# Last layer of a three-stage kernel: the Newton operations one turn later, conversions spread over the turns, row sums a turn earlier

## The chip, the core and the metric

The kernel runs on one core of a Trainium2 chip. The metric is the device time of one execution in microseconds; the time before is the median of three runs. A core has engines that run side by side and wait for one another through semaphores: TensorE (PE; PEld is its weight load), VectorE (DVE), ScalarE (ACT), GpSimd (POOL), and SyncE (SP), which here only issues transfers. Each engine works through its own list of instructions in the order in which the program gives them.

## What is computed

Attention with a window, a mixture of eight experts on its output, and a last dense layer on that. All the changes are in the last layer, which for 1536 tokens of width 512 computes

```
h = x @ w_in                                             # 512 -> 2048
sp = np.where(h > 20.0, h, np.log1p(np.exp(np.minimum(h, 20.0))))
g = h * np.tanh(sp)
out = g @ w_out                                          # 2048 -> 512
```

The inputs x are the sums of two rows per token that the experts left in memory, each with its weight. The weights w_in and w_out come as 64-bit numbers and are turned on the chip into pairs of a high and a low part; likewise every operand of a product has a high and a low part (`whi`/`wlo`, `xgh`/`xgl`, `hhi`/`hlo`), and a product is three matmuls (high by high, high by low, low by high).

## The kernel before

**Tiling.** The last layer takes the tokens in four blocks (`tb`) of 384 (`TB`) and the 2048 hidden columns in 16 pieces (`f`) of 128. A pair (tb, f) is a step; there are 64, numbered from 0. `last_in` does a step's first product: 12 matmuls of 384 columns into a PSUM tile `hp`, of which there are three. `last_out` does its second product: six matmuls with `hhi` and three with `hlo`, of 512 columns, added up over the 16 steps of a block in three PSUM tiles `ac`.

**Between the two products** a step has a chain on ScalarE and VectorE: `mish_0` Exp of hp into v (L1178, ScalarE); `mish_1` a minimum that keeps v in range (L1182, VectorE), Square into s (L1183) and Ln into r (L1184), both ScalarE; `mish_2` Exp of -r (L1188, ScalarE), a first value of a reciprocal; `mish_3` three operations on VectorE (L1193 to L1195), one Newton step and the product with h; below they are the Newton trio. `mish_5` copies the result into `hhi` (L1198, ScalarE) and `mish_6` takes the low part `hlo` (L1201, VectorE).

**Order.** The order is written out by hand: the loop at L1243 makes 66 turns, and each engine's list follows the code. Turn n emits the first product of step n, the second product of step n-2, and from the chain L1178, L1182 to L1188 and the trio of step n together with the copy and the low part of step n-1. The first and last step are cut in thirds.

**Work beside it.** In turns 2 to 13 the last six halves of weights are converted, one half in two turns: L327 and L328 in the even turn, L329 and L330 in the odd one, and at the end of the odd turn `rest` with a copy on ScalarE (L322) and L323 and L324 on VectorE. In blocks 0 to 2 the next block's inputs are made: GpSimd gathers the rows (`rows_of`, L868), `combine_2` scales one on ScalarE (L1153) and adds the other on VectorE (L1154), in turns f = 5, 9, 13; `combine_3` transposes the sum on TensorE (L1159) and splits it into high (L863, ScalarE) and low (L864, VectorE), in turns f = 6, 10, 14. All of that stands at the end of its turn, behind the trio. After a block `last_store` copies the results out (L1236 on ScalarE, L1234 on VectorE).

**Line numbers** are those of the kernel before; in the changed kernel these operations stand 8 to 10 lines further on (L1154 is L1164 there, L1193 is L1203, L864 is L874, and the conversion's L327, L328, L329, L330, L322, L323, L324 are L335, L336, L337, L338, L327, L330, L331).

Of the kernel before, what the change touches and what calls it, by code (L numbers as in the profile page):

```python
# [21 lines left out]
P = 128  # L22
# [154 lines left out]
def build(tc, ctx, I, out, n_global, n_local, dbg=None):  # L177
# [118 lines left out]
    def w64_load():  # L296
        j, s = divmod(state["load64"], 2)
        if j < 16:
            state["load64"] += 1
            raws[j, s] = wraw.tile([P, 512, 2], I32, name="raw")  # L300
            nc.sync.dma_start(raws[j, s], I["w_moe2"][j, :, s * 512:(s + 1) * 512].bitcast(I32)
                              .rearrange("p (a b) -> p a b", b=2))

    def w64_begin():


        j, s = divmod(state["conv"], 2)
        if j == 16:
            return None
        state["conv"] += 1  # L310
        if s == 0:
            pool, n = (wlast, "l") if j < 16 - RING else (wring, "")
            pieces[64 + j] = (pool.tile([P, 1024], F32R, name="whi" + n), pool.tile([P, 1024], F32R, name="wlo" + n))
        raw = raws.pop((j, s))
        lw, uw = raw[:, :, 0], raw[:, :, 1]
        hi, lo = (w[:, s * 512:(s + 1) * 512] for w in pieces[64 + j])
        t1 = wtmp.tile([P, 512], I32, name="t1", bufs=2)
        t2 = wtmp.tile([P, 512], I32, name="t2", bufs=1)
        f1 = t1.bitcast(F32)

        def rest():
            A.activation(hi, f1, AF.Copy)  # L322
            V.tensor_tensor(f1, f1, hi.bitcast(F32), op=OP.subtract)  # L323
            V.tensor_tensor(lo, f1, lo.bitcast(F32), op=OP.add)  # L324

        return (
            lambda: V.tensor_scalar(t1, uw, 0x07FFFFFF, 3, op0=OP.bitwise_and, op1=OP.logical_shift_left),  # L327
            lambda: V.scalar_tensor_tensor(t1, uw, -0x40000000, t1, op0=OP.bitwise_and, op1=OP.bitwise_or),  # L328
            lambda: V.tensor_scalar(t2, t1, -0x800000, None, op0=OP.bitwise_and),  # L329
            lambda: V.scalar_tensor_tensor(lo, lw.bitcast(U32), 2.0 ** -52, t2.bitcast(F32), op0=OP.mult, op1=OP.mult),  # L330
            rest,  # L331
        )

    xgs, xgT = {}, {}
# [836 lines left out]


    def mish_begin(hp, n):
        r = mk.tile([P, TB], F32, name="r", bufs=1)
        return hp, vt[:, n % 2, :TB], vt[:, 2 + n % 2, :TB], r

    def mish_0(m, cc):
        A.activation(m[1][:, cc], m[0][:, cc], AF.Exp)  # L1178
# [11 lines left out]
    def mish_3(m, cc):  # L1190

        h, v, s, r = (a[:, cc] for a in m)
        V.scalar_tensor_tensor(s, s, 1.0, r, op0=OP.add, op1=OP.mult)  # L1193
        V.scalar_tensor_tensor(s, s, -2.0, r, op0=OP.add, op1=OP.mult)
        V.scalar_tensor_tensor(v, s, 0.5, h, op0=OP.add, op1=OP.mult)  # L1195

    def mish_5(m, g, cc):
        A.activation(g[0][:, cc], m[1][:, cc], AF.Copy)  # L1198

    def mish_6(m, g, cc):  # L1200
        V.tensor_tensor(g[1][:, cc], m[1][:, cc], g[0][:, cc].bitcast(F32), op=OP.subtract)  # L1201

    def mish_end():  # L1203
        return tuple(mk.tile([P, CAP], F32R, name=n)[:, :TB] for n in ("hhi", "hlo"))
# [4 lines left out]
    def for_cuts(n, stage, *a):  # L1209

        for cc in (THIRDS if n in (0, 16 * NTB - 1) else [ALL]):
            stage(*a, cc)
# [26 lines left out]

    steps = [(tb, f) for tb in range(NTB) for f in range(16)]  # L1240
    m = {}
    vt = mk.tile([P, 4, CAP], F32, name="yT", bufs=1)
    for n in range(len(steps) + 2):  # L1243
        new, old = n < len(steps), 1 <= n <= len(steps)
        if new:
            tb, f = steps[n]
            m[n] = mish_begin(last_in(tb, f), n)
        if n >= 2:
            last_out(*steps[n - 2])
        if n % 2 == 0:  # L1250
            half = w64_begin() if n else None
        if new:
            for_cuts(n, mish_0, m[n])
        if old:
            g = gT[steps[n - 1]] = mish_end()
        if old:
            for_cuts(n - 1, mish_5, m[n - 1], g)
        if new:
            for_cuts(n, mish_1, m[n])
        if half:  # L1260
            half[n % 2 * 2]()
        if new:
            for_cuts(n, mish_2, m[n])
        if old:
            for_cuts(n - 1, mish_6, m[n - 1], g)
        if half:
            half[n % 2 * 2 + 1]()
        if new:
            for_cuts(n, mish_3, m[n])
        if late and n:  # L1270
            late.pop(0)()
        if half and n % 2:
            half[4]()
        if n >= 2:
            last_store(*steps[n - 2])
        if new and tb + 1 < NTB:
            for c in range(TC):
                t = TC * (tb + 1) + c
                if f == 2 + 4 * c:
                    rows[t] = [rows_of(t, 0), rows_of(t, 1)]  # L1280
                if f == 5 + 4 * c:
                    combine_2(t, rows[t])
                if f == 6 + 4 * c:
                    combine_3(t, rows[t], ps_q, "tq")
        if n % 2:
            w64_load()

# [107 lines left out]
```

## Time and profile before

| | us |
|---|---|
| median of 3 runs | 741.88 (741.67 to 742.07) |
| the profiled execution: its time | 742.57 |
| its span in the trace | 740.8 |
| TensorE busy, whole span | 707.8 (96%) |
| VectorE busy | 524.5 (71%) |
| ScalarE busy | 421.7 (57%) |

The span is what the trace covers of the profiled execution; its own time is 1.8 us more. Times below count from the span's start. Busy time of TensorE says that a matmul was under way; where matmuls follow each other closely they overlap in the trace, so the pace is read from their starts. The last layer begins at 444.86 us and takes the last 40% of the span.

### The profile page before, as it was taken

What the parts mean: (1) busy time and instruction counts of PE and PEld (TensorE: products, weight loads), DVE (VectorE), ACT (ScalarE), POOL (GpSimd) and SP (SyncE); (2) the same over time, 40 slices, a digit from 0 to 9 for tenths busy, and PEclk for the clock granted to TensorE, in tenths of its full rate; (3) what the DMA queues carried; (4) which work ended last, traced back from release to release, by engine and by line L of the source; (5) the groups of instructions that cost most, each with busy time, mean ns of one, the idle gap of its engine ahead of it and who ended that gap; (6) DMA issues with size and microseconds to landing.
All of it is one profiled execution on the core that took longest, in us unless ns stands there. A gap on an engine that the chain in (4) does not pass through costs nothing.

```text
span 740.8 us, 11706 instructions
## 1 busy us (share of the span) xinstructions
PE 707.8 (96%) x4259; PEld 642.3 (87%) x4259; DVE 524.5 (71%) x1237; ACT 421.7 (57%) x892; POOL 64.0 (9%) x83
## 2 busy tenths in 40 slices
PE   7999899999999999999999999898999999999994
PEld 4777778899999999999999988787989989989993
DVE  7789769877676675857576886888666666666653
ACT  5999632435354444444354447566767677676663
POOL 2000200301011010101000032100020020000000
PEclk9999899999999999999999999899999999999998
DMA  7799421757565565646454643300120030001001
GB/s 163 205 230 240 125 66 42 227 163 229 160 213 165 197 199 167 193 151 220 140 195 142 213 160 130 116 29 0 47 83 1 0 104 12 0 1 43 2 0 47
DMA packets 42932, 89.26 MB, mean 120 GB/s; under 512 B 5987, under 2 KB 18403, under 8 KB 42868
## 3 DMA queue, kind: packets, MB, share of 16 engines
q1 hardware_dynamic: 35412, 69.37, 30.7%
q0 software_dynamic: 4096, 13.11, 6.0%
q10 hardware_dynamic: 3360, 5.97, 2.2%
q8 instruction: 35, 0.57, 0.3%
q14 instruction: 29, 0.24, 0.1%
HBM read 75.32 MB, written 13.11 MB: 119 GB/s over the span
## 4 chain that ended last, share of the span: by engine, by line
PE 72%; DVE 14%; ACT 8%; issue 2%; DMA 2%; POOL 1%; ACTq 0%; DVEq 0%
PE hp L858 10%; PE hp L859 10%; PE hp L860 10%; PE ac L859 5%; PE ac L858 5%; PE ac L860 5%; PE ac L1222 5%; PE ac L1223 5%; PE ac L1227 4%; PE xp L567 3%; PE sp L516 3%; PE tp L554 3%; DVE wlo L280 2%; PE tq L892 2%; ACT r L1184 1%
## 5 line engine op out<-in xcount | busy, mean ns | idle before, releaser
L858 PE MATMUL hp<-xgh,whi 128*128 128x416 f32 (+1 forms) x288 | 104.3, 362 | 0.0
L860 PE MATMUL hp<-xgh,wlo 128*128 128x416 f32 (+1 forms) x288 | 100.8, 350 | 0.0
L859 PE MATMUL hp<-xgl,whi 128*128 128x416 f32 (+1 forms) x288 | 100.6, 349 | 0.2 <-DVE xgl L711 0.2
L280 DVE TENSOR_TENSOR wlo<-raw,whi 128x1024 fp32r<-128x1024 f32 x61 | 74.7, 1224 | 35.9 <-ACT whi L277 35.3
L858 PE MATMUL ac<-hhi,whi 128*128 128x416 f32 x256 | 91.7, 358 | 0.0
L859 PE MATMUL ac<-hlo,whi 128*128 128x416 f32 x256 | 90.0, 352 | 1.2 <-DVE hlo L905 1.2
L860 PE MATMUL ac<-hhi,wlo 128*128 128x416 f32 x256 | 89.9, 351 | 0.0
L1193 DVE SCALAR_TENSOR_TENSOR yT<-yT,r 128x384 f32<-128x384 f32 (+1 forms) x68 | 36.4, 535 | 73.8 <-ACT r L1188 69.8
L858 PE MATMUL hp<-xgh,whil 128*128 128x384 f32 x224 | 77.2, 344 | 0.0
L859 PE MATMUL hp<-xgl,whil 128*128 128x384 f32 x224 | 76.4, 341 | 0.0
L860 PE MATMUL hp<-xgh,wlol 128*128 128x384 f32 x224 | 76.1, 340 | 0.0
L277 ACT ACTIVATE whi<-raw 128x1024 fp32r<-128x1024 f32 x61 | 64.3, 1055 | 9.4 <-ACT ys L940 6.8
L904 ACT ACTIVATE hhi<-hp 128x416 fp32r<-128x416 f32 x64 | 32.6, 509 | 51.1 <-PE hp L860 48.7
L1222 PE MATMUL ac<-whil,hhi 128*128 128x512 f32 x144 | 57.6, 400 | 1.6 <-ACT hhi L1198 1.3
L1178 ACT ACTIVATE yT<-hp 128x384 f32<-128x384 f32 (+1 forms) x68 | 31.6, 471 | 47.5 <-PE hp L860 45.6
L1223 PE MATMUL ac<-wlol,hhi 128*128 128x512 f32 x144 | 56.8, 394 | 0.0
L859 PEld LDWEIGHTS hp<-xgl,whi 128*128 128x128 f32 x288 | 54.3, 189 | 1.1 <-DVE xgl L711 0.4
L858 PEld LDWEIGHTS hp<-xgh,whi 128*128 128x128 f32 x288 | 54.2, 188 | 1.1 <-ACT xgh L710 0.4
L860 PEld LDWEIGHTS hp<-xgh,wlo 128*128 128x128 f32 x288 | 54.0, 188 | 0.5
L322 ACT ACTIVATE whil<-t 128x512 fp32r<-128x512 f32 x26 | 16.5, 633 | 66.2 <-DVE t L328 56.3
L341 POOL DMA_INDIRECT xg<-xd,gidx x32 | 32.7, 1023 | 227.1 <-PE tq L892 192.8
L905 DVE SCALAR_TENSOR_TENSOR hlo<-hp,hhi 128x416 fp32r<-128x416 f32 x64 | 37.5, 586 | 18.6 <-ACT hhi L904 18.4
(241 smaller groups left out, 1528.8 us busy)
## 6 DMA issues: line engine op xcount, KB each, us to landing
raw<-in_w_moe SPq DMA_DIRECT2D x96, 512.0 KB
yd<-ys ACTq DMA_DIRECT2D x21, 256.0 KB
ks<-in_k_t SPq DMA_DIRECT2D x24, 136.0 KB
qr<-in_q_t SPq DMA_DIRECT2D x24, 128.0 KB
vt<-in_v_w SPq DMA_DIRECT2D x12, 256.0 KB
xd<-xs SPq DMA_DIRECT2D x12, 256.0 KB
out<-ys SPq DMA_DIRECT2D x12, 256.0 KB
vt<-in_v_w SPq DMA_DIRECT2D x10, 208.0 KB
```

Of the source, the lines that this page charges most:

```text
L277: A.activation(hi, raw, AF.Copy)
L280: e_lo.tensor_tensor(lo, raw, hi.bitcast(F32), op=OP.subtract)
L341: G.indirect_dma_start(out=xg[:n], out_offset=None, in_=xd[:1 + blocks * P], in_offset=bass.IndirectOffsetOnAxis(ap=idx, axis=0))
L858: T.matmul(ps, whi, xhi, start=first, stop=False)
L859: T.matmul(ps, whi, xlo, start=False, stop=False)
L860: T.matmul(ps, wlo, xhi, start=False, stop=last)
L904: A.activation(hhi, hp[:, :CAP], AF.Relu)
L905: V.scalar_tensor_tensor(hlo, hp[:, :CAP], 0.0, hhi.bitcast(F32), op0=OP.max, op1=OP.subtract)
L1178: A.activation(m[1][:, cc], m[0][:, cc], AF.Exp)
L1193: V.scalar_tensor_tensor(s, s, 1.0, r, op0=OP.add, op1=OP.mult)
L1222: T.matmul(acc2[tb][c], ghi[:, cc], whi, start=(f == 0), stop=False)
L1223: T.matmul(acc2[tb][c], ghi[:, cc], wlo, start=False, stop=False)
```

## The change

The trio of step n-1 is emitted in turn n, behind Exp (L1178) and ahead of the copy `hhi`, the next conversion and the minimum. The conversions become single operations that `convert` takes from a queue: one behind the trio in every turn from 1 on, and one, in every third turn two, behind the low part; the copy L322 is emitted just ahead of the operation that follows it. A new half begins, and the next half's load is issued, when the queue is empty. `combine_2` moves from f = 5, 9, 13 to f = 4, 8, 12; `combine_3` stays, and both still stand at the end of their turn. The tiles change with it: one v for all steps, s in two alternating places, r in one of two, and the trio's result in s.

```
         def rest():
+            high()
+            for op in low:
+                op()
+
+        def high():
             A.activation(hi, f1, AF.Copy)
-            V.tensor_tensor(f1, f1, hi.bitcast(F32), op=OP.subtract)
-            V.tensor_tensor(lo, f1, lo.bitcast(F32), op=OP.add)
+
+        low = (
+            lambda: V.tensor_tensor(f1, f1, hi.bitcast(F32), op=OP.subtract),
+            lambda: V.tensor_tensor(lo, f1, lo.bitcast(F32), op=OP.add),
+        )
...
     def mish_begin(hp, n):
-        r = mk.tile([P, TB], F32, name="r", bufs=1)
-        return hp, vt[:, n % 2, :TB], vt[:, 2 + n % 2, :TB], r
+        r = vt[:, 3, :TB] if n % 2 else mk.tile([P, TB], F32, name="r", bufs=1)
+        return hp, vt[:, 0, :TB], vt[:, 1 + n % 2, :TB], r
...
-        V.scalar_tensor_tensor(v, s, 0.5, h, op0=OP.add, op1=OP.mult)
+        V.scalar_tensor_tensor(s, s, 0.5, h, op0=OP.add, op1=OP.mult)
...
+    def convert(k):
+
+        for _ in range(k):
+            if not todo:
+                half = w64_begin()
+                if not half:
+                    return
+                w64_load()
+                todo.extend((*half[:2], *half[5:6], *half[2:4], *half[6:]))
+            while todo:
+                op = todo.popleft()
+                op()
+                if op.__name__ != "high":
+                    break
...
-        if n % 2 == 0:
-            half = w64_begin() if n else None
         if new:
             for_cuts(n, mish_0, m[n])
         if old:
+            for_cuts(n - 1, mish_3, m[n - 1])
+        convert(1 if n else 0)
+        if old:
             g = gT[steps[n - 1]] = mish_end()
-        if old:
             for_cuts(n - 1, mish_5, m[n - 1], g)
         if new:
             for_cuts(n, mish_1, m[n])
-        if half:
-            half[n % 2 * 2]()
-        if new:
             for_cuts(n, mish_2, m[n])
         if old:
             for_cuts(n - 1, mish_6, m[n - 1], g)
-        if half:
-            half[n % 2 * 2 + 1]()
-        if new:
-            for_cuts(n, mish_3, m[n])
+        convert((1 + (n % 3 == 0)) if n else 0)
         if late and n:
             late.pop(0)()
-        if half and n % 2:
-            half[4]()
...
-                if f == 5 + 4 * c:
+                if f == 4 + 4 * c:
                     combine_2(t, rows[t])
...
-        if n % 2:
-            w64_load()
```

What that does to the engines' lists shows at two places. In the names `yT` holds v and s, `ys` and `xg` the two rows of a token, `t_...` the conversion's temporaries, `tq` the transposed sum. First, VectorE around the first row sum (turn 5 before, turn 4 now); before:

```order
L1193 SCALAR_TENSOR_TENSOR yT<-yT,r 128x384
L1194 SCALAR_TENSOR_TENSOR yT<-yT,r 128x384
L1195 SCALAR_TENSOR_TENSOR yT<-yT,hp 128x384
L323 TENSOR_TENSOR t_5397<-t_5397,whi 128x512
L324 TENSOR_TENSOR wlo<-t_5397,wlo 128x512
L1154 SCALAR_TENSOR_TENSOR ys<-ys,wlh,xg 128x512
L1182 TENSOR_SCALAR yT<-yT 128x384
L327 TENSOR_SCALAR t_5482<-raw 128x512
L1201 TENSOR_TENSOR hlo<-yT,hhi 128x384
```

and now:

```order
L1192 TENSOR_SCALAR yT<-yT 128x384
L1211 TENSOR_TENSOR hlo<-yT,hhi 128x384
L337 TENSOR_SCALAR t_5368<-t_5367 128x512
L1164 SCALAR_TENSOR_TENSOR ys<-ys,wlh,xg 128x512
L1203 SCALAR_TENSOR_TENSOR yT<-yT,r 128x384
L1204 SCALAR_TENSOR_TENSOR yT<-yT,r 128x384
L1205 SCALAR_TENSOR_TENSOR yT<-yT,hp 128x384
L338 SCALAR_TENSOR_TENSOR wlo<-raw,t_5368 128x512
L1192 TENSOR_SCALAR yT<-yT 128x384
L1211 TENSOR_TENSOR hlo<-yT,hhi 128x384
```

The sum of rows (L1154, now L1164) stood behind its turn's trio and stands ahead of it now; of the conversion one operation is left between trio and minimum.

On ScalarE, in the same two turns, from the last Exp on; before:

```order
L1188 ACTIVATE r<-r 128x384
L322 ACTIVATE whi<-t_5397 128x512
L1153 ACTIVATE xg<-xg,wlh 128x512
L1178 ACTIVATE yT<-hp 128x384
L1198 ACTIVATE hhi<-yT 128x384
```

and now:

```order
L1198 ACTIVATE r<-r 128x384
L327 ACTIVATE whi<-t_5367 128x512
L1163 ACTIVATE xg<-xg,wlh 128x512
L1188 ACTIVATE yT<-hp 128x384
L1208 ACTIVATE hhi<-yT 128x384
```

Only the line numbers differ here: the scaling of the row (L1153, now L1163) stays behind the Exp that the trio needs, and behind the conversion's copy.

Second, VectorE at the first split of a transposed sum, in turn 6 of both kernels; before:

```order
L1193 SCALAR_TENSOR_TENSOR yT<-yT,r 128x384
L1194 SCALAR_TENSOR_TENSOR yT<-yT,r 128x384
L1195 SCALAR_TENSOR_TENSOR yT<-yT,hp 128x384
L864 TENSOR_TENSOR xgl<-tq,xgh 128x4x128
L1182 TENSOR_SCALAR yT<-yT 128x384
```

and now:

```order
L335 TENSOR_SCALAR t_5486<-raw 128x512
L336 SCALAR_TENSOR_TENSOR t_5486<-raw,t_5486 128x512
L874 TENSOR_TENSOR xgl<-tq,xgh 128x4x128
L1203 SCALAR_TENSOR_TENSOR yT<-yT,r 128x384
L1204 SCALAR_TENSOR_TENSOR yT<-yT,r 128x384
L1205 SCALAR_TENSOR_TENSOR yT<-yT,hp 128x384
L337 TENSOR_SCALAR t_5487<-t_5486 128x512
L1192 TENSOR_SCALAR yT<-yT 128x384
```

The split's low half (L864, now L874) has gone ahead of the trio as well, and two conversion operations with it.

## Rows read from the trace of the kernel before

**Rows 1.** Windows, first block: start:end us, us, busy PE PEld DVE ACT POOL, clock

```profile
444.86:521.75 76.89, 68.96 (x334) 60.47 (x332) 61.30 (x130) 50.35 (x104) 6.90 (x6) 0.96 0.20 66
```

**Rows 2.** Waits of PE, 444 to 522 us: who, for whom, us, times, longest

```profile
PE tq L1159 <- DVE ys L1154: 6.4, 3, 3.2
```

**Rows 3.** Timeline, PE: start us, us, what; second products of steps 16 and 46

```profile
532.25 0.39 PE L1222 MATMUL ac<-whil,hhi 128*128 128x512 f32 x1
...
660.69 0.39 PE L1222 MATMUL ac<-whi,hhi 128*128 128x512 f32 x1
```

**Rows 4.** Chain that ended last, in order of time: one set of transposes

```profile
551.24 0.44 PE tq L1159 x4
```

**Rows 5.** Timeline, step 16 to 17: the plain cycle, VectorE and ScalarE

```profile
527.64 0.56 DVE L1193 SCALAR_TENSOR_TENSOR yT<-yT,r 128x384 f32<-128x384 f32 x1 [1.16 <-ACT r L1188]
...
529.29 0.35 DVE L1182 TENSOR_SCALAR yT<-yT 128x384 f32<-128x384 f32 x1
529.41 0.53 ACT L1198 ACTIVATE hhi<-yT 128x384 fp32r<-128x384 f32 x1 [0.69 <-DVE yT L1195]
...
531.12 0.53 ACT L1188 ACTIVATE r<-r 128x384 f32<-128x384 f32 x1
...
531.68 0.56 DVE L1193 SCALAR_TENSOR_TENSOR yT<-yT,r 128x384 f32<-128x384 f32 x1 [1.16 <-ACT r L1188]
```

**Rows 6.** Timeline, turns 5 and 6: conversion and row sum, ScalarE and VectorE

```profile
472.13 0.53 ACT L1188 ACTIVATE r<-r 128x384 f32<-128x384 f32 x1
...
472.56 0.62 ACT L322 ACTIVATE whi<-t 128x512 fp32r<-128x512 f32 x1
...
473.09 0.70 ACT L1153 ACTIVATE xg<-xg,wlh 128x512 f32<-128x512 f32 x1
...
475.68 0.74 DVE L1154 SCALAR_TENSOR_TENSOR ys<-ys,wlh,xg 128x512 f32<-128x512 f32 x1
476.34 0.35 DVE L1182 TENSOR_SCALAR yT<-yT 128x384 f32<-128x384 f32 x1
...
476.61 0.42 DVE L327 TENSOR_SCALAR t<-raw 128x512 int32<-128x512 int32 x1
...
476.94 0.55 DVE L1201 TENSOR_TENSOR hlo<-yT,hhi 128x384 fp32r<-128x384 f32 x1
...
478.58 0.56 DVE L1193 SCALAR_TENSOR_TENSOR yT<-yT,r 128x384 f32<-128x384 f32 x1 [0.48 <-ACT r L1188]
```

**Rows 7.** Timeline: trio of step 1; a copy hhi, the matmul waiting for it

```profile
455.29 0.56 DVE L1193 SCALAR_TENSOR_TENSOR yT<-yT,r 128x384 f32<-128x384 f32 x1 [1.29 <-ACT r L1188]
...
470.42 0.52 ACT L1198 ACTIVATE hhi<-yT 128x384 fp32r<-128x384 f32 x1 [1.43 <-DVE yT L1195]
...
471.00 0.50 PE L1222 MATMUL ac<-whil,hhi 128*128 128x512 f32 x1 [0.34 <-ACT hhi L1198]
```

**Rows 8.** Timeline: a late copy hhi, its matmul; the matmul of the last step

```profile
711.56 0.52 ACT L1198 ACTIVATE hhi<-yT 128x384 fp32r<-128x384 f32 x1
...
715.13 0.40 PE L1222 MATMUL ac<-whil,hhi 128*128 128x512 f32 x1
...
728.62 0.50 PE L1222 MATMUL ac<-whi,hhi 128*128 128x512 f32 x1 [0.79 <-ACT hhi L1198]
```

**Rows 9.** Timeline: the split of a transposed sum, VectorE and ScalarE

```profile
520.75 0.68 DVE L864 TENSOR_TENSOR xgl<-tq,xgh 128x512 fp32r<-128x512 f32 x1
521.35 0.35 DVE L1182 TENSOR_SCALAR yT<-yT 128x384 f32<-128x384 f32 x1
...
655.24 0.58 ACT L863 ACTIVATE xgh<-tq 128x512 fp32r<-128x512 f32 x1
```

**Rows 10.** Timeline, GpSimd: second gather of the first pair of rows

```profile
459.91 0.95 POOL L868 DMA_INDIRECT xg<-yd,cidx  x1 [0.30 <-issue]
```

**Rows 11.** Windows after TensorE's longest stop; the clock stands behind the engines

```profile
475.00:480.00 5.00, 3.52 (x13) 3.53 (x14) 4.41 (x10) 2.24 (x4) 0.00 (x0) 0.53 0.02 9
480.00:485.00 5.00, 5.00 (x22) 4.49 (x21) 3.40 (x8) 3.19 (x6) 0.00 (x0) 0.79 0.03 7
```

More of the change, by code (lines that the diff above doesn't have):

```diff
@@ L331, in w64_begin @@
             rest,
+            high,
+            *low,
         )
@@ L1194, in mish_3 @@
         V.scalar_tensor_tensor(s, s, -2.0, r, op0=OP.add, op1=OP.mult)
-        V.scalar_tensor_tensor(v, s, 0.5, h, op0=OP.add, op1=OP.mult)
+        V.scalar_tensor_tensor(s, s, 0.5, h, op0=OP.add, op1=OP.mult)
     def mish_5(m, g, cc):
-        A.activation(g[0][:, cc], m[1][:, cc], AF.Copy)
+        A.activation(g[0][:, cc], m[2][:, cc], AF.Copy)
     def mish_6(m, g, cc):
-        V.tensor_tensor(g[1][:, cc], m[1][:, cc], g[0][:, cc].bitcast(F32), op=OP.subtract)
+        V.tensor_tensor(g[1][:, cc], m[2][:, cc], g[0][:, cc].bitcast(F32), op=OP.subtract)
     def mish_end():
@@ L1241, in build @@
     m = {}
+    todo = deque()
+    def convert(k):
[11 more added lines that the diff above has]
+                    break
     vt = mk.tile([P, 4, CAP], F32, name="yT", bufs=1)
```

## The prediction

> **What bounds the kernel now.** I read the stretches first. In the first block of the last layer TensorE is busy 68.96 of 76.89 us [rows 1]; it is in this block, with the last weight conversions, that it stands still. The waits view names the cause: 6.4 us in three waits, for the row sum L1154 on VectorE [rows 2]. After that block it never stops until the very end. So I need two clocks, TensorE's own pace and the pace of the chain on ScalarE and VectorE, and how far the one may fall behind the other.
>
> TensorE's pace: the second product of step 16 begins at 532.25 and that of step 46 at 660.69, 128.44 us for 30 steps with six sets of transposes [rows 3] at 0.44 [rows 4], so 4.19 per step.
>
> The chain's pace [rows 5]: from a Newton trio's start to the next one's it is 4.04. Its parts: trio to the copy hhi 1.77; hhi to the start of the last Exp 1.71; Exp to the next trio 0.56 (0.53 long, hence a hand-over of 0.03). A second branch runs from the trio over the minimum: 1.65 from trio to minimum, and 2.24 from minimum to the next trio [rows 6], together 3.89. What VectorE does between trio and minimum lengthens this branch; what it does between minimum and trio lies in the shadow of Square, Ln and Exp, and is free while it fits in 2.24.
>
> The slack: TensorE takes hhi 0.58 after that copy began [rows 7]. Step 16's trio starts at 527.64, so hhi would serve from 527.64 + 1.77 + 0.58 = 529.99, and is taken at 532.25 [rows 3, 5]: 2.26 of slack. Late in the layer it is 715.13 - 711.56 - 0.58 = 2.99 [rows 8], all that the order of the steps gives.
>
> **The change part by part.** *Conversions.* Each half has two short operations (0.33 from start to start) [rows 6] and four long ones (0.60, taken from L864, of the same shape) [rows 9]. Before, the last two stood between trio and minimum and the other four in the shadow. Now one per turn stands between trio and minimum, and one or two in the shadow, where the minimum (0.27 to the next start), the low part (0.55 long) and at most two long ones leave room in 2.24. From step 1's trio to step 16's there are 15 cycles, 5 with a short operation (3.89 + 0.33 = 4.22) and 10 with a long one (3.89 + 0.60 = 4.49): 21.1 + 44.9 = 66.0. The first conversion comes a turn earlier, ahead of step 1's minimum: 0.33 more.
>
> A row bears on the seams here: L864 lasts 0.68, and the next operation starts 0.60 after it [rows 9], so VectorE begins one while the last still writes. The Trainium skill, VectorE: DVE Perf Modes, section The DRAIN you can't avoid, says that the next operation waits until the pipe is empty, with an exception for one that is not held. By the plain rule a conversion between trio and minimum would cost 0.08 more, 1.2 us over 15 turns; by the row nothing, and the trace sides with the exception.
>
> *The trio a turn on.* Its place in the chain is the same: after the Exp, ahead of the next minimum. What changes is that all that a turn emits at its end now stands ahead of it. For conversions and the store's copy L1234 that is the shadow. For the rows it is not. L1154 needs L1153, which stands on ScalarE behind this turn's Exp; L864 needs L863, which stands there too. Both used to run on ScalarE while VectorE did the trio, and VectorE's half cost its own time after it. Now VectorE, which works in order, waits at L1154 or L864 for ScalarE, and the trio, whose input has been ready, is queued behind; behind the trio are hhi, the minimum and the next Square.
>
> The price per row sum: Exp to the next ScalarE operation 0.43, L1153 0.70 with the hand-over 0.03, L1154 0.66 until the next [rows 6]: 1.82 against 0.56, so 1.26. Twice (turns 4 and 12) a conversion's copy L322 stands ahead of L1153: 0.53 more [rows 6]. The price of L863 and L864: 0.43 + 0.58 + 0.03 + 0.60 - 0.56 = 1.08 [rows 9]. No row shows this wait itself, since before it was hidden. Its lower bound is VectorE's half alone fitting the shadow, 0; its upper bound adds a late gather. The hand-over is taken from the Exp that releases a trio, the nearest row.
>
> In the first block: 3 x 1.26 + 2 x 0.53 + 3 x 1.08 = 8.1. So step 16's trio starts at 455.29 [rows 7] + 0.33 + 66.0 + 8.1 = 529.7, against 527.64 [rows 5]: 2.1 later. That is just the slack of 2.26, which is now used up: TensorE stands at step 16 where it stood, give or take 0.2. Its waits for L1154 and the cold clock go, and waits for hhi come in their place.
>
> In blocks 2 and 3 there are six pairs. The chain takes 30 x 4.04 + 6 x (1.26 + 1.08) = 135.2 from step 16's trio to step 46's. TensorE wants 128.44, and with no slack left it follows the chain. Step 46's hhi is taken at 529.7 + 135.2 + 1.77 + 0.58 = 667.3 instead of 660.69 [rows 3]: 6.6 later, in pieces of about 1 us after each pair.
>
> From step 46 to step 63 no rows are summed. The chain gains 4.19 - 4.04 = 0.15 a step, 17 times, 2.55 of the 2.99. The last step's hhi, for which TensorE waits already [rows 8], is so 0.4 later. A first matmul after a stop takes 0.50 for 0.39 [rows 7], 0.1 once, since the chain sets the pace else.
>
> *Row sums moved up a turn.* The transposes no longer wait for L1154: that is the 6.4 us [rows 2], already counted as replaced. The gathers are not held by the turn: the first pair is issued by 459.91 [rows 10], and L1153 now comes at about 469, so I take no wait for them. *Weight loads* are issued when a half begins, some 2.6 turns ahead of use, and go past the late store in SP's queue; raw is free by then, and I take 0. *Fewer buffers* (one v, r in the spare slot): the next Exp may overwrite v once ScalarE's own Square has read it, in order; 0. hp is held one turn longer, but has three buffers, and TensorE asks for the same one two turns after that; 0.
>
> Sum: 0 in the first block, 6.6 in blocks 2 and 3, 0.4 + 0.1 at the end: **+7.1 us**. On the profiled execution's own 742.57 (span 740.8 and 1.8 around it) that is 749.7; it lies 0.7 above the median of the runs, 741.88, from which the forecast is **749.0**.
>
> **The rivals.** *The pair costs VectorE's time only* (the other side). If ScalarE's half is done when VectorE comes to it, a pair costs 0.66 + 0.60 = 1.26 instead of 2.34 at most. Then step 16's trio is at 529.7 - 3.2 = 526.5, TensorE is 1.1 + 2.2 = 3.3 ahead, and blocks 2 and 3 run at TensorE's pace (30 x 4.04 + 6 x 1.26 = 128.8): 741.9 - 3.3 = 738.6. It decides from about 1.6 per pair: 3 x 0.74 is gained in the first block and 6 x 0.74 in the others, 6.6 in all. For it speaks only that no row shows the wait; against it, that L1153 and L863 stand behind the Exp on ScalarE in both orders.
>
> *The clock falls again.* After a wait of 3.2 us [rows 2] the granted clock fell to 0.53 and then 0.79 [rows 11], between the 1.2 and the 2.4 GHz level; by those rows it cost 3.5 x 0.47 + 5 x 0.21 = 2.7 us. My stalls in the first block are up to 2 us, every second turn. If they are enough, 2.7 to 5 us come on top where TensorE and not the chain is late: 749.0 + 2.7 = 751.7 up to 754. The Trainium skill, TensorE: Matmul & The Clock Gate, section A second HAM failure mode: psum-queue depth-cycling, says that frequent short idling between groups of matmuls makes the clock swing; no row here shows it without a long stop. It speaks against this rival that the chain sets the pace there.
>
> *The loss is smaller, since I count in full something that is partly hidden:* if half of ScalarE's part is hidden, a pair costs some 1.8, nine times 0.54 less: 744.1, and up to 746.5 for less of it.
>
> **How the numbers follow.** My forecast has 0.72, the clock 0.08, the smaller loss 0.08, the gain 0.12. The forecast's own range is 746.5 to 751.5. Stretched over the smaller loss and most of the clock's case it is 744.0 to 753.5, with the gain left out. A measurement of this kernel tells about 0.2%, 1.5 us, from no change. Faster by more: 0.12; within: 0.03; slower: 0.85.
>
> **What would show it.** In the waits of the changed kernel, L1154 and L864 wait for L1153 and L863, nine times each, about 0.7 and 0.6 us; TensorE's waits for L1154 are gone, and it waits for hhi about 1 us after each pair in blocks 2 and 3. Cycles between trios are 4.04 plain, 4.2 or 4.5 with a conversion, 5.1 and 5.3 with a row's half. It would be wrong if TensorE runs through blocks 2 and 3 without a stop, if VectorE is not found waiting ahead of the trio in the nine turns, or if step 16's trio starts well before 528.

## The result, and the profile after

| | before | after |
|---|---|---|
| median | 741.98 us (741.56 to 743.45) | 750.34 us (749.30 to 751.97) |
| ratio to before | | 1.0108 (95% interval 1.0095 to 1.0122) |
| the profiled execution: its time, its span | 742.57, 740.8 | 750.62, 748.8 |
| TensorE, VectorE, ScalarE busy | 707.8, 524.5, 421.7 | 712.0, 525.6, 416.8 |

The change makes the kernel 8.4 us slower; 749.0 was forecast, in a range of 744.0 to 753.5. VectorE and ScalarE are busy for nearly the same time as before, so what was added there is waiting. TensorE shows 4.2 us more; how far that is work is said below.

The chain that ended last, followed back over the whole span, by engine (a line of each kernel's page), before and then after:

```profile
PE 72%; DVE 14%; ACT 8%; issue 2%; DMA 2%; POOL 1%; ACTq 0%; DVEq 0%
```

```profile
PE 50%; DVE 23%; ACT 20%; issue 4%; DMA 1%; POOL 1%; ACTq 0%; DVEq 0%
```

TensorE's share falls from 72% to 50%. The chain between the two products now sets the pace over a stretch in which TensorE set it.

Waits of VectorE and of TensorE in the last layer of the changed kernel, 444 to 748 us: who, for whom, us, times, longest; the two kinds that are new on VectorE, and TensorE's two largest.

```profile
DVE ys L1164 <- ACT xg L1163: 15.8, 9, 2.2
DVE xgl L874 <- ACT xgh L873: 13.2, 9, 1.6
...
PE ac L1232 <- ACT hhi L1208: 8.9, 9, 1.8
PE ac L1232 <- ACT ys L1246: 3.7, 3, 1.5
```

VectorE waits nine times each for ScalarE's half of a sum and of a split. The transposes' wait for the sum [rows 2] is gone; TensorE waits for `hhi` instead, and, which I had not foreseen, for a copy of the store. Not all of VectorE's 15.8 and 13.2 us are a loss, since part of it would have been spent waiting for the last Exp anyway; the price is read from the cycle of the chain. Timeline of the changed kernel in block 1, trio to trio, ScalarE and VectorE:

```profile
541.91 0.56 DVE L1203 SCALAR_TENSOR_TENSOR yT<-yT 128x384 f32<-128x384 f32 x1 [1.16 <-ACT yT L1194]
...
545.40 0.53 ACT L1198 ACTIVATE r<-r 128x384 f32<-128x384 f32 x1
545.83 0.71 ACT L1163 ACTIVATE xg<-xg,wlh 128x512 f32<-128x512 f32 x1
546.57 0.75 DVE L1164 SCALAR_TENSOR_TENSOR ys<-ys,wlh,xg 128x512 f32<-128x512 f32 x1 [1.77 <-ACT xg L1163]
...
547.24 0.55 DVE L1203 SCALAR_TENSOR_TENSOR yT<-yT,r 128x384 f32<-128x384 f32 x1
...
551.28 0.56 DVE L1203 SCALAR_TENSOR_TENSOR yT<-yT 128x384 f32<-128x384 f32 x1 [1.16 <-ACT yT L1198]
...
554.77 0.53 ACT L1198 ACTIVATE r<-r 128x384 f32<-128x384 f32 x1
555.20 0.58 ACT L873 ACTIVATE xgh<-tq 128x512 fp32r<-128x512 f32 x1
555.81 0.69 DVE L874 TENSOR_TENSOR xgl<-tq,xgh 128x512 fp32r<-128x512 f32 x1 [1.64 <-ACT xgh L873]
556.42 0.55 DVE L1203 SCALAR_TENSOR_TENSOR yT<-yT,r 128x384 f32<-128x384 f32 x1
```

The trio could start 0.56 after its Exp, at 545.96 (compare [rows 5]). VectorE stands at L1164 until ScalarE has scaled the row behind that Exp, and the trio starts at 547.24. The cycle with a sum is 547.24 - 541.91 = 5.33, the one with a split 556.42 - 551.28 = 5.14, and the plain one between them 551.28 - 547.24 = 4.04: 1.29 and 1.10 for the two halves of a pair.

Timeline of the changed kernel: first matmul of the layer, trio and second product of step 16, the same of step 46, the last matmul; behind it the last matmul of the kernel before.

```profile
444.42 0.42 PE L868 MATMUL hp<-xgh,whil 128*128 128x384 f32 x1
...
529.77 0.56 DVE L1203 SCALAR_TENSOR_TENSOR yT<-yT,r 128x384 f32<-128x384 f32 x1 [1.43 <-ACT r L1198]
...
532.12 0.50 PE L1232 MATMUL ac<-whil,hhi 128*128 128x512 f32 x1
...
665.36 0.55 DVE L1203 SCALAR_TENSOR_TENSOR yT<-yT,r 128x384 f32<-128x384 f32 x1
...
667.70 0.50 PE L1232 MATMUL ac<-whi,hhi 128*128 128x512 f32 x1
...
740.20 0.40 PE L1235 MATMUL ac<-whi,hlo 128*128 128x512 f32 x1
```

```profile
731.61 0.40 PE L1225 MATMUL ac<-whi,hlo 128*128 128x512 f32 x1
```

Against [rows 3]: step 16's product stands 0.13 earlier than before (0.3 later, counted from the layer's first matmul), step 46's 7.0 later, and the last matmul 8.6 later.

### The profile page after: what moved, and what is told of

Its sections match the earlier page's. It is cut to its first block, busy times and chain, and to the rows that moved or that the text cites. A ratio compares the mean times of both kernels' runs of the same rounds, so it can differ in the third digit from the quotient of the medians.

```text
span 748.8 us, 11639 instructions
## 1 busy us (share of the span) xinstructions
PE 712.0 (95%) x4259; PEld 639.3 (85%) x4259; DVE 525.6 (70%) x1237; ACT 416.8 (56%) x892; POOL 63.7 (9%) x83
## 4 chain that ended last, share of the span: by engine, by line
PE 50%; DVE 23%; ACT 20%; issue 4%; DMA 1%; POOL 1%; ACTq 0%; DVEq 0%
PE hp L868 6%; PE hp L869 6%; PE hp L870 6%; PE ac L869 5%; PE ac L868 5%; PE ac L870 5%; ACT yT L1193 4%; DVE yT L1204 4%; DVE yT L1203 4%; DVE yT L1205 3%; PE xp L577 3%; PE tp L564 3%; ACT hhi L1208 2%; PE sp L526 2%; ACT yT L1194 2%
## 5 line engine op out<-in xcount | busy, mean ns | idle before, releaser
L869 PE MATMUL hp<-xgl,whi 128*128 128x416 f32 (+1 forms) x288 | 100.6, 349 | 0.2 <-DVE xgl L721 0.2
L869 PE MATMUL ac<-hlo,whi 128*128 128x416 f32 x256 | 90.0, 352 | 1.2 <-DVE hlo L915 1.2
L1208 ACT ACTIVATE hhi<-yT 128x384 fp32r<-128x384 f32 (+1 forms) x68 | 34.4, 506 | 78.2 <-DVE yT L1205 76.7
L869 PE MATMUL hp<-xgl,whil 128*128 128x384 f32 x224 | 76.1, 340 | 0.3 <-DVE xgl L874 0.3
L869 PEld LDWEIGHTS hp<-xgl,whi 128*128 128x128 f32 x288 | 54.3, 189 | 1.1 <-DVE xgl L721 0.4
L327 ACT ACTIVATE whil<-t 128x512 fp32r<-128x512 f32 x26 | 16.5, 633 | 66.3 <-DVE t L336 59.3
L869 PEld LDWEIGHTS ac<-hlo,whi 128*128 128x128 f32 x256 | 48.1, 188 | 2.4 <-DVE hlo L915 1.9
```

The source lines that it names most:

```text
L869: T.matmul(ps, whi, xlo, start=False, stop=False)
L1208: A.activation(g[0][:, cc], m[2][:, cc], AF.Copy)
```

## The experiments

The theory: a row sum and a split, emitted ahead of the trio, make VectorE wait for ScalarE's half, which stands behind the Exp that the trio waits for; the trio, ready, is queued behind that. The rivals: the spread conversions or the trio's new place cost the time; or the move of the sums by a turn does; or VectorE's own time for the halves does.

All times below stand beside runs of the kernel before on the same chip (741.51, 740.92 and 742.10 us in the three groups), and the ratios compare with those. The last two columns are read from the profiled execution and count from the layer's first matmul, since the stages before the layer vary by some 2 us from one execution to another: for the changed kernel 532.12 - 444.42 = 87.7 and 740.20 - 444.42 = 295.8.

| kernel | us | ratio (95% interval) | step 16's product | last matmul |
|---|---|---|---|---|
| before | 741.98 | 1 | 87.4 | 286.8 |
| after | 750.34 | 1.0108 (1.0095 to 1.0122) | 87.7 | 295.8 |
| e1: both halves in the shadow | 738.59 | 0.9960 (0.9941 to 0.9979) | 85.5 | 285.2 |
| e2: both halves behind the trio | 739.70 | 0.9974 (0.9962 to 0.9986) | 86.1 | 285.4 |
| e3: sums a turn back | 749.25 | 1.0104 (1.0083 to 1.0124) | 87.1 | 295.2 |
| e4: before, sums a turn up | 741.31 | 0.9991 (0.9977 to 1.0005) | 88.4 | 287.7 |
| e5: two store copies on VectorE | 749.49 | 1.0119 (1.0101 to 1.0137) | 88.0 | 294.8 |
| e6: e1, rows a turn earlier | 734.67 | 0.9916 (0.9898 to 0.9934) | 79.9 | 282.0 |
| e7: after, row scaled twice | 755.36 | 1.0194 (1.0174 to 1.0214) | 90.0 | 302.8 |
| e8: before, row scaled twice | 740.42 | 0.9993 (0.9982 to 1.0004) | 86.2 | 285.5 |
| e9: e6, two store copies on VectorE | 733.98 | 0.9893 (0.9874 to 0.9912) | 79.9 | 280.1 |
| e10: sum alone in the shadow | 739.84 | 0.9967 (0.9952 to 0.9982) | 83.1 | 284.3 |
| e11: split alone in the shadow | 744.12 | 1.0029 (1.0014 to 1.0045) | 87.2 | 289.0 |

Some times lie just outside the range written before the run where the outcome is the one forecast: e2 and e6 by 0.2 above it, e3, e7 and e8 by 0.1 to 0.8 below it. The kernel before itself differs by 1.2 us among the three groups, so the ratios weigh more than the last tenths of a time. The real misses are e1, e4 and e10; they are taken up below.

### e1: VectorE's halves kept back into the next turn's shadow

```
-        split_ps(x2T[tb][0][:, :, c * P:(c + 1) * P], x2T[tb][1][:, :, c * P:(c + 1) * P], tp)
+        hi, lo = (w[:, :, c * P:(c + 1) * P] for w in x2T[tb])
+        A.activation(hi, tp, AF.Copy)
+        op = lambda: V.tensor_tensor(lo, tp, hi.bitcast(F32), op=OP.subtract)
+        op() if behind is None else behind.append(op)
...
-        V.scalar_tensor_tensor(rows[1], rows[1], wlh[:, 1, t:t + 1], rows[0], op0=OP.mult, op1=OP.add)
+        behind.append(lambda: V.scalar_tensor_tensor(rows[1], rows[1], wlh[:, 1, t:t + 1], rows[0], op0=OP.mult, op1=OP.add))
...
             for_cuts(n - 1, mish_6, m[n - 1], g)
+        while behind:
+            behind.popleft()()
```

> The changed kernel, except that VectorE's halves of the row sums (L1164 and L874) are kept back by a turn and emitted behind the next turn's low part, in the shadow of Square, Ln and Exp; ScalarE's halves (L1163, L873) stay at the end of their turn. Theory (the loss is VectorE waiting for ScalarE ahead of the trio): the nine pairs cost the chain nothing in blocks 2 and 3 and little in the first (two conversions and a row's half are 0.27 + 0.55 + 1.20 + 0.66 = 2.7 us in a shadow of 2.24, so up to 0.4 in the turns where that comes together). Step 16's trio then starts near 522 (455.2 + 66 + about 1), its second product near 525, TensorE runs through blocks 2 and 3 without a stop, and the time is about 734 us (733 to 736): faster than both kernels. Rival A (the loss comes from the spread conversions or from the trio's new place itself): the time stays near 750. Rival B (the pair's own VectorE time counts, not its wait): about 738.6 or below, not to be told from the theory by this run alone; the next run does that.

Measured 738.59: 11 us less than the changed kernel by the ratios, and a little faster than the one before. Rival A falls: conversions and trio stand as in the changed kernel, and the loss is gone. But 734 it is not. TensorE's longest stop in e1 (L869 is the matmul with `xgl`; L892 is L874 there), and two windows with and behind it, with the granted clock in the column before the last two:

```profile
516.52 0.69 PE L869 MATMUL hp<-xgl,whil 128*128 128x384 f32 x1 [2.60 <-DVE xgl L892]
...
515.00:520.00 5.00, 3.48 (x11) 3.49 (x12) 4.84 (x10) 2.03 (x4) 0.00 (x0) 0.57 0.01 3
520.00:525.00 5.00, 5.00 (x21) 4.34 (x20) 2.59 (x5) 2.66 (x5) 0.00 (x0) 0.75 0.00 0
```

The last split of a block is needed by the next block's first matmuls; kept back by a turn it comes too late, TensorE stops for 2.60 us, and the clock is low for the ten us behind. Both together are some 6.0 us. That is what e6 takes away.

### e2: the halves behind the trio

The loop that empties `behind` stands right behind the trio of the next turn, ahead of the conversion and the minimum, so that VectorE's own time for them stays on the path.

> As the run before, but the halves kept back are emitted right behind the next turn's trio, between trio and minimum, so that each still costs VectorE's own time on the way from trio to minimum, while ScalarE's half is long done. Theory: a pair costs 0.66 + 0.60 = 1.26 us at most, less 0.15 of it for each half where the other branch (4.04 against 3.89) is the longer: step 16's trio at about 525 to 526, no stop of TensorE in blocks 2 and 3, and about 738 us (736.5 to 739.5). If VectorE's own time were the price and not the wait, this kernel would be as slow as the changed one, 750; if neither counts, it would be as fast as the run before, 734.

Measured 739.70, 0.2 above the range that I gave. This is the rival "a pair costs VectorE's time only" of the prediction, built: it comes to a gain of 0.26%, the price with the wait to a loss of 1.08%. The wait, not the work, is what costs. The gain is even understated: as in e1 the last split of the first block comes late, TensorE stops for 1.44 us for it, and the granted clock is 0.98 and 0.68 in the ten us around and behind that stop, which is no part of the rival. From step 16's product to step 46's e2 takes 128.4 us, as the kernel before does.

### e3 and e4: the move of the sums by a turn, undone and alone

```
-                if f == 4 + 4 * c:
+                if f == 5 + 4 * c:
                     combine_2(t, rows[t])
```

(e3, in the changed kernel; e4 has the reverse in the kernel before.)

> The changed kernel with the row sums (L1163, L1164) back in turns f = 5, 9, 13; Newton trio and conversions as changed. Theory: the price of a pair to the chain does not hang on the turn it stands in, so the cycles between trios keep their sums, the chain still sets the pace through blocks 2 and 3, and TensorE's wait for L1164 at the transposes comes back only where TensorE is not late anyway: 750 to 752 us. Rival (moving the row sums up is what costs): below 746.

> The kernel before with only the row sums moved up, to turns f = 4, 8, 12. Theory: VectorE's half stands behind its trio there and costs its own time; TensorE's 6.4 us of waits for the row sum in the first block go, with the low clock after them (2.7 us by the windows), but the chain paces TensorE in that block nearly as much, so that only part is gained: 735 to 741 us. If the chain was not late in that block before: the full 9 us, 733. Rival (the move itself costs): 744 or more.

Measured 1.0104 against 1.0108, and 0.9991: in either order of the trio this part changes nothing that can be told. For e3 that was forecast (its ratio is within the changed kernel's interval, its time 0.75 below the range that I gave): TensorE's wait for the sum is back, 5.3 us in five places, at no cost that shows. For e4 I had expected up to 6 us of gain, and got none that can be told from zero. The waits of TensorE in e4 and three windows show what takes its place:

```profile
PE ac L1222 <- ACT hhi L1198: 3.3, 8, 0.8
PE hp L859 <- DVE xgl L864: 1.5, 1, 1.5
PE hp L858 <- ACT xgh L863: 0.9, 1, 0.9
...
515.00:520.00 5.00, 2.64 (x10) 1.60 (x9) 3.51 (x8) 3.45 (x7) 0.00 (x0) 0.88 0.00 0
520.00:525.00 5.00, 5.00 (x16) 4.61 (x15) 2.71 (x6) 3.03 (x7) 0.00 (x0) 0.50 0.01 3
525.00:530.00 5.00, 5.00 (x25) 4.42 (x24) 2.42 (x5) 2.39 (x5) 0.00 (x0) 0.94 0.00 0
```

The 6.4 us for the sum [rows 2] are gone. In their place come 3.3 us for `hhi` (some of it in the layer's first steps and its last) and 2.4 us for the third split, with a clock as low as 0.50 behind them: 5 x 0.12 + 5 x 0.50 + 5 x 0.06 = 3.4 us. So the work on ScalarE and VectorE was as late as TensorE in that block. The sizes hold for this execution alone: at 743.69 it is the slowest of the ten of e4, 2.4 us above their median.

### e7 and e8: the dose, ScalarE's half made longer

```
         A.activation(rows[0], rows[0], AF.Copy, scale=wlh[:, 0, t:t + 1])
+        A.activation(rows[0], rows[0], AF.Copy)
```

> The changed kernel with one more ScalarE operation per row sum: a copy of the scaled row onto itself behind L1163 (0.70 us each, nine of them). Theory (VectorE waits for ScalarE's half ahead of the trio, and the trio for VectorE): each goes onto the chain in full, and the chain has no slack left, so 9 x 0.70 = 6.3 us: about 756.6 (755.5 to 757.5). Rival (ScalarE's half is not on the path; the loss comes from VectorE's own work ahead of the trio): under 752.

> The kernel before with the same extra copy behind L1153. Theory: there ScalarE scales the row while VectorE does the trio, 0.43 + 0.70 + 0.70 + 0.03 = 1.86 us behind the Exp's start against 0.56 + 1.77 = 2.33 for the trio's end, so the extra copy is hidden: 741.5 (740.5 to 742.5). Rival (0.70 us of ScalarE costs its time wherever it stands): about 747.8.

The same nine copies cost 0.86% (1.0194 less 1.0108, 6.4 us of 742) in the changed kernel and nothing (0.9993, the interval holds 1) in the one before. In the trace the last matmul of e7 comes 302.8 - 295.8 = 7.0 us later, of which 1.1 is the clock's (below). VectorE's wait in e7, one cycle with a sum, and TensorE's last stop and last matmul (line numbers are one up behind the added line):

```profile
DVE ys L1165 <- ACT xg L1164: 21.8, 9, 2.9
...
615.92 0.56 DVE L1204 SCALAR_TENSOR_TENSOR yT<-yT 128x384 f32<-128x384 f32 x1 [1.16 <-ACT yT L1199]
...
619.84 0.71 ACT L1163 ACTIVATE xg<-xg,wlh 128x512 f32<-128x512 f32 x1
620.58 0.63 ACT L1164 ACTIVATE xg<-xg 128x512 f32<-128x512 f32 x1
621.25 0.75 DVE L1165 SCALAR_TENSOR_TENSOR ys<-ys,wlh,xg 128x512 f32<-128x512 f32 x1 [2.44 <-ACT xg L1164]
621.91 0.55 DVE L1204 SCALAR_TENSOR_TENSOR yT<-yT,r 128x384 f32<-128x384 f32 x1
...
742.83 0.69 PE L1236 MATMUL ac<-whi,hlo 128*128 128x512 f32 x1 [0.77 <-DVE hlo L1212]
...
745.45 0.63 PE L1236 MATMUL ac<-whi,hlo 128*128 128x512 f32 x1
```

The cycle is 621.91 - 615.92 = 5.99, 0.66 more than 5.33, and the wait grows from 15.8 to 21.8, 0.67 for each of nine. Nine times 0.66 is 5.9. The seven matmuls from that last stop on take 745.45 - 742.83 = 2.62 in e7 and 740.20 - 738.71 = 1.49 in the changed kernel: in e7 they ran at a low clock, with single matmuls of 0.63 for 0.40. Without that the 7.0 are 5.9 as well. What is put on ScalarE between the Exp and the sum goes on the path one for one, but only where the sum stands ahead of the trio. This is the run that shows the mechanism most directly.

### e10 and e11: one half each

e10 keeps back the sum's half alone, e11 the split's.

> The changed kernel with only the row sum's VectorE half (L1164) kept back into the next turn's shadow; the split (L873, L874) stays as changed, ahead of the trio. Theory (prices add up: 1.26 and twice 0.53 more for the sum, 1.08 for the split): the first block's chain is 3 x 1.26 + 2 x 0.53 = 4.8 shorter and all that starts step 16 comes 4.8 earlier; in blocks 2 and 3 the chain needs 30 x 4.04 + 6 x 1.08 = 127.7 against TensorE's 128.4, so TensorE sets the pace there. From the start of the layer step 16's second product comes at 87.7 - 4.8 = 82.9 (87.4 in the kernel before), then as in the kernel before: 4.5 us less than that, about 737 (735.5 to 738.5). Rival (the prices do not add, the two waits share one cause): 742 or more.

> The changed kernel with only the split's low half (L874) kept back into the next turn's shadow; the sum L1164 stays ahead of the trio. Theory: in blocks 2 and 3 the chain needs 30 x 4.04 + 6 x 1.26 = 128.8 against TensorE's 128.4, nearly even. In the first block the chain gains 3 x 1.08, but the third split comes 2.9 us behind its high part, as in the run with both in the shadow, so that the first matmul with xgl of step 16 stands about where it stands in the changed kernel, with a stop of about 2.6 us and up to 2.2 us of low clock behind it: step 16's second product at 88 to 90 us from the start of the layer, against 87.4 in the kernel before. In all 1 to 3 us more than the kernel before: 742.5 to 745.5. Rival (prices do not add): 747 or more.

On the chain the prices add up: in e10 step 16's product comes at 83.1 from the start of the layer (82.9 was worked out), and from there TensorE runs at its own pace but for one stop. In time the two halves don't add, since TensorE's own pace is the floor. The time of e10 is 2.3 us below the kernel before and not 4.5; of what is missing 1.5 is a wait for a copy of the store at step 16, the same as in e6 (below). That takes 739.84 above the range that I gave. In e11 the time is within the range, 2.0 us above the kernel before, but step 16's product is at 87.2, not 88 to 90: the stop there was 1.18 and not 2.6. In place of that, blocks 2 and 3 lost more than forecast, since the split that is kept back makes TensorE stop at each change of blocks:

```profile
590.95 0.44 PE L869 MATMUL hp<-xgl,whil 128*128 128x384 f32 x1 [0.95 <-DVE xgl L892]
...
660.55 0.44 PE L869 MATMUL hp<-xgl,whil 128*128 128x384 f32 x1 [0.95 <-DVE xgl L892]
```

### e5: the store's copies

In the changed kernel TensorE waits 1.46, 1.14 and 1.15 us for L1246, in the second product of a block's first step (16, 32, 48). There ScalarE's two copies of the finished block stand behind the last Exp of a lagging chain. The tiles `ac` come from four buffers in turn, so the next block's second tile is the finished block's first, and the first of ScalarE's two copies frees it. The expectations of e5 and e9 speak of another copy; the edit takes the right one, the first, off ScalarE: two of the three copies are then VectorE's.

```
-                if c % 2:
+                if c < 2:
                     V.tensor_scalar(os, acc2[tb][c], 2.0, None, op0=OP.mult)
```

> The changed kernel with the second and the third of a block's store copies the other way round: two of three on VectorE instead of two on ScalarE (the first and second on VectorE, the third on ScalarE). Theory: at a change of blocks TensorE waits for the last ScalarE copy (L1246), which stands behind the lagging chain's Exp (1.46, 1.14 and 1.15 us in the trace of the changed kernel); the wait that comes after step 46's chain has no more row sums behind it and is not given back, so that taking the second copy off ScalarE gains about 1.2 us: about 749, with TensorE's waits for L1246 down from 3.7 us to under 1.5. Rival (the lag there is given back at the end, because the last hhi is what TensorE waits for): no change of the time, 750 to 751.

The trace shows the effect, the times don't settle it. Timeline at the last change of blocks, in the changed kernel with ScalarE's two copies (the stop ends with the first of them, at 677.36 + 0.58, and not with the second), then in e5, and the last matmul of e5:

```profile
677.36 0.58 ACT L1246 ACTIVATE ys<-ac 128x512 f32<-128x512 f32 x1
677.84 0.59 ACT L1246 ACTIVATE ys<-ac 128x512 f32<-128x512 f32 x1
...
677.99 0.50 PE L1232 MATMUL ac<-whil,hhi 128*128 128x512 f32 x1 [1.15 <-ACT ys L1246]
```

```profile
675.89 0.50 PE L1232 MATMUL ac<-whil,hhi 128*128 128x512 f32 x1 [0.18 <-DVE ys L1244]
...
738.22 0.40 PE L1235 MATMUL ac<-whi,hlo 128*128 128x512 f32 x1
```

From step 46's product to the last matmul the changed kernel takes 740.20 - 667.70 = 72.5, e5 738.22 - 666.61 = 71.6, the kernel before 731.61 - 660.69 = 70.9. That is 0.9 of the 1.2 expected. The ratios, 1.0108 and 1.0119, don't differ by more than their intervals, about 1 us to either side; so the gain in time stays open, and is at most about 1 us in this kernel.

### e6 and e9: the rows a turn earlier, and the stores

```
-                if f == 2 + 4 * c:
+                if f == 1 + 4 * c:
                     rows[t] = [rows_of(t, 0), rows_of(t, 1)]
-                if f == 4 + 4 * c:
+                if f == 3 + 4 * c:
                     combine_2(t, rows[t], behind)
-                if f == 6 + 4 * c:
+                if f == 5 + 4 * c:
                     combine_3(t, rows[t], ps_q, "tq", behind)
```

(e6, on top of e1; e9 adds e5's line.)

> The kernel with the row sums' VectorE halves in the shadow, and all work on the rows another turn earlier: gathers at f = 1, 5, 9, L1163 at 3, 7, 11, transposes and L873 at 5, 9, 13. Theory: with the halves in the shadow the chain no longer set the pace; what was left was the first matmul with xgl of step 16, which waited 2.60 us for the last split, and the clock at 0.57 and 0.75 in the ten us behind it (5 x 0.43 + 5 x 0.25 = 3.4 us). A turn earlier the split is done about 4 us before TensorE asks for it, both go, and the time is 738.6 - 6.0 = 732.6 (731.5 to 734.5). Rival (something else of the chain is the bound there, or the rows arrive too late for an L1163 in turn 3): 737 or more.

> The kernel with all row work a turn earlier and VectorE's halves in the shadow, and in addition a block's first two store copies on VectorE, the third on ScalarE. Theory: there TensorE is no longer late through the chain, and its only wait between the first steps and the last is 1.47 us at 524.70, for the third store copy on ScalarE; with that copy one place earlier in ScalarE's order the wait falls to about 0.2 and the time by about 1.3: 733.4 on a chip where the kernel without this edit takes 734.7 (ratio to the kernel before 0.990). Rival (the chain is the bound at that place as well, and the wait turns into one for hhi): no change, ratio 0.992.

In e6 the stop for `xgl` and the low clock behind it are gone, and step 16's product comes 5.6 us earlier than in e1 (6.0 expected). Of that 3.1 reach the last matmul. One stop has come in its place, of 1.5 us for the store's copy again; and in this execution the last seven matmuls ran at a low clock, as in e7, 724.67 - 722.06 = 2.61 for 1.5. The time, 734.67, is 0.2 above the range that I gave. The store's wait and the last window of TensorE in e6, then the same wait in e9:

```profile
PE ac L1235 <- ACT ys L1249: 1.5, 1, 1.5
...
720.00:725.00 5.00, 3.68 (x9) 2.34 (x9) 3.02 (x11) 1.53 (x4) 0.00 (x0) 0.72 0.14 52
```

```profile
PE ac L1235 <- DVE ys L1247: 0.5, 1, 0.5
```

With two copies on VectorE 0.5 of the 1.5 us is left. e9 is at 0.9893, 8.0 us faster than the kernel before and 16 faster than the changed one: the lowest time of the kernels measured. Its step over e6 (0.9916) is 1.7 us by the ratios, with intervals that overlap a little. In the traces e9's last matmul is 2.0 earlier, of which 1.1 is the low clock at the end of e6, and 0.9 the stop; so the two traces show a gain of about 0.9, and not the 1.3 that I gave.

## Why the prediction was right, and where it was off

**The price of a pair** was the term on which all rested, and no row of before showed it. Worked out were 1.26 and 1.08; measured are 1.29 and 1.10. Where a conversion's copy L327 stands ahead as well, 1.26 + 0.53 on a cycle of 4.49 gives 6.28; the trace has 470.43 - 464.12 = 6.31:

```profile
464.12 0.56 DVE L1203 SCALAR_TENSOR_TENSOR yT<-yT 128x384 f32<-128x384 f32 x1 [0.36 <-ACT yT L1198]
470.43 0.55 DVE L1203 SCALAR_TENSOR_TENSOR yT<-yT,r 128x384 f32<-128x384 f32 x1
474.93 0.56 DVE L1203 SCALAR_TENSOR_TENSOR yT<-yT 128x384 f32<-128x384 f32 x1 [0.81 <-ACT yT L1198]
```

The next cycle, with a long conversion alone, is 4.50 (4.49 worked out). Step 16's trio was forecast at 529.7 and starts at 529.77, the 15 cycles before it adding up to 74.6 for 74.4, so this is no luck of one term against another. What was misread are the waits that should show it: "about 0.7 and 0.6 us" each were forecast, and they are 15.8 / 9 = 1.76 and 13.2 / 9 = 1.47, since VectorE comes to the half before the last Exp has ended, for which it waits 1.16 in a plain cycle too.

**The slack used up, and blocks 2 and 3.** Step 16's product was to stand where it stood, give or take 0.2, and does. From its trio to step 46's the chain takes 665.36 - 529.77 = 135.6 (135.2 forecast), and step 46's product stands at 667.70 (667.3). So 6.6 became 7.0. One detail was wrong: TensorE does not stop for 1 us after each pair. It stops longer at a few places and falls behind in pieces too small to show as stops elsewhere. The windows of the changed kernel for block 1 and block 2, TensorE's busy time behind the length:

```profile
521.75:589.60 67.85, 65.56 (x327) 57.40 (x326) 43.82 (x87) 42.65 (x82) 5.91 (x6) 1.00 0.12 36
589.60:658.70 69.10, 67.16 (x336) 59.32 (x335) 43.15 (x85) 43.66 (x85) 5.21 (x5) 1.00 0.10 31
```

Only 2.3 + 1.9 = 4.2 of the 7.0 are idle; the rest must lie in matmuls that start later than their pace while the one before still shows as busy, which would also explain why TensorE's busy time grew. A stage's loss is better read from the starts of the same matmul in two traces than from idle time.

**The tail was the term that failed.** I gave 0.4 + 0.1 us from step 46 to the end; it is 72.5 - 70.9 = 1.6. Of the stores I had looked at VectorE's copy, which is in the shadow, and not at ScalarE's (L1236, now L1246), which stands behind an Exp that comes later when the chain lags. It makes TensorE stop for 1.15 us at 677.99, where no pair follows that would have made it stop anyway. At the first change of blocks the same stop, 1.46, costs next to nothing, since the chain sets the pace behind it: without it and the one of step 32, in e5, the stretch from step 16's product to step 46's takes 135.2 for 135.6.

Where the 1.6 lie shows from one step's product to the next. From step 48 to 49 it is 673.23 - 669.07 = 4.16 before, 681.81 - 676.22 = 5.59 after and 679.85 - 675.08 = 4.77 in e5. From step 49 to 63 it is 55.39, 55.40 and 55.38: behind the change of blocks nothing is lost. So the 0.4 + 0.1 forecast did not show, for TensorE, made late by the stop, leaves the chain time to catch up. By my estimate the chain then has 2.99 - 1.43 = 1.56 us to make good, some ten steps at 0.15; and the chain's cycles are 4.04 to 4.05 for ten steps, from 665.36 to 705.83, and 4.1 to 4.2 behind. That e5's tail is 0.7 longer than before, near the 0.5 forecast, is chance. The tail does not hang on one execution: up to the last seven matmuls, where the clock can be low, it is 71.0 in the changed kernel, e3 and e7, and 69.4 in the kernel before and in e1, e2, e4, e6 and e8 to e11, where the chain does not lag at that place.

**The rivals.** "VectorE's time only" was priced at 738.6; e2, which is that case built, takes 739.7 with a stop of 1.44 us of its own. The smaller loss, from a partly hidden wait, is excluded by the cycles and by e7, where each added piece is paid in full. The clock rival came in part: the fall was milder than the 2.7 us that I had allowed for: in the windows behind TensorE's stop of 1.82 us before 472.77 it was

```profile
470.00:475.00 5.00, 3.18 (x14) 2.49 (x13) 4.12 (x9) 2.49 (x6) 0.00 (x0) 0.93 0.19 64
475.00:480.00 5.00, 5.00 (x22) 4.55 (x22) 4.05 (x9) 3.16 (x7) 0.00 (x0) 0.73 0.11 41
```

which is 5 x 0.07 + 5 x 0.27 = 1.7 us in a block whose end the chain sets. That it cost nothing in the end is argued, from step 16's product being where it was, and not shown by a run of its own.

**Which part of the change did it.** The trio's move to the next turn, together with what is left standing ahead of it. The move of the sums by a turn is worth nothing either way (e3, e4). With the wait out of the way (e2), the trio's move and the spread conversions are together a gain of 0.26%, and with the halves in the shadow and the rows early enough (e6) of 0.84%. No run has the trio's move without the spread conversions, so what each of the two is worth stays open.

## What to carry to other kernels

When an operation moves from the end of one turn into the next, list everything that its engine emits between the old place and the new: each of these now stands ahead of it, and one that needs another engine costs the wait for that engine, not its own time. Where a job has a half on each of two in-order engines, put the second half a turn behind the first, in a place where its engine waits anyway, and start the whole job early enough that its last user isn't made late. Before counting a wait as gained, ask what would have been late at the same place without it; here 6.4 us of waiting could be removed (e4) for no gain at all.

## What the runs showed of the hardware that I had not expected

The granted clock after a stop of TensorE can't be told from the stop's length. After 3.2 us it fell to 0.53 in the kernel before [rows 2, 11], after 2.60 to 0.57 in e1. But in e8 TensorE stood still for 3.11 us ahead of 474.71, for the same reason as in the kernel before, and the clock stayed at its full level of 2.4 GHz. The stop, and two windows of e8, the clock again before the last two columns:

```profile
474.71 0.66 PE L1160 MATMUL tq<-ident,ys 128*128 128x128 f32 x4 [3.11 <-DVE ys L1155]
...
470.00:475.00 5.00, 1.89 (x10) 1.23 (x9) 4.34 (x9) 3.46 (x8) 0.00 (x0) 1.00 0.30 105
475.00:480.00 5.00, 5.00 (x29) 4.59 (x28) 4.44 (x10) 3.77 (x7) 0.00 (x0) 1.00 0.00 0
```

In e7 a stop of 2.49 us left it at 1.00 as well, while the two short ones of e4, 0.91 and 1.45 close together, brought 0.50. All thirteen traces have the same two stops, of 0.76 to 0.80 us each, ahead of the last seven matmuls, and only in e6 and e7 did these run at a low clock. Such stops therefore cost between nothing and 3.4 us beyond their own length. The ten executions of e1 lie 5.6 us apart, the fastest (735.73) with a mean granted clock of 0.993, the slowest two (741.29, 741.28) with 0.988 and 0.985; that the clock makes part of that spread is likely, and no run varies it alone. A term for the clock belongs in the range, not in the sum.
